# One semaphore for all products of TensorE, and a plan with other costs, in a fused attention and gated feed-forward kernel

## The chip, the cores and the metric

The kernel runs on one core of a Trainium2 chip. The metric is the device time of one execution in microseconds (us), as the median of several runs. Before the change it is 720.37 us, the median of three runs (720.32 to 722.3).

## What is computed

One input x, 2048 rows of 512 numbers in bf16, goes through two branches, and a gate mixes them row by row:

```python
    x = A_x
    g = _sigmoid((x * gate_w).sum(-1, keepdims=True))
    a = _A_ref(x, A_wqkv, A_wo)
    b = _B_ref(x, B_w_gate, B_w_up, B_w_down)
    return g * a + (1 - g) * b
```

Branch a is attention with 32 heads of 16 numbers each, without a mask: q, k and v are products of x with wqkv, the scores of each head are q·k / 4, the softmax runs over all 2048 keys, and the result is multiplied with wo. Branch b is a feed-forward block of width 1376 whose hidden row is the plain product of two projections, (x·w_gate) times (x·w_up), multiplied with w_down.

## The kernel before, in words

**Tiles.** The attention is cut into 2048 score tiles. One tile holds 128 keys against 512 queries for one head, 128 x 512 numbers in one PSUM bank. Four heads and 512 queries make a group `m`; a group has 16 key blocks times 4 heads, 64 tiles, and there are 32 groups. TensorE computes a score tile with four products of 64 rows and 32 columns that run beside each other in one row half of the array (`score`, lines 1173 to 1239, the products on L1219). The other row half (64 rows) works on another tile at the same time. The same form, four products on one row half, serves P·V (`pv_pack`, L1662) and the projections and the feed-forward block ("fills", `tile4`, L554). A few early products use the whole array (L550, L588).

**The exponential** is done in two ways. ScalarE takes most tiles with an ACTIVATE that reads one, two or three neighbouring banks and writes bf16 into cells of the SBUF buffer PT (`act_policy`, lines 1265 to 1323, L1314): a single, a pair or a triple. VectorE takes the others (`dve_pass`, L1378): one TENSOR_SCALAR turns the scores into int16 numbers whose bits, read as bf16, approximate the exponential. To even out the error, three shifted copies of each such tile are made in PT (L1330 on GpSimd, L1331 on VectorE), and P·V runs over all four with V scaled to match. The scaled V copies are made once (L735). Banks 0 to 3 belong to the tiles of ScalarE, banks 4 to 7 to all the rest. `want_d` and `score` decide which engine a tile goes to.

**Other work.** VectorE moves projections out of PSUM (KT L629, QR L686, V L745), multiplies the feed-forward halves (L905, L920), and copies each finished group's P·V result to SBUF (`oraw`, L1601). `norm` (from L1493) then divides by the softmax's sum: the sums go by DMA from `oraw` to `den4`, VectorE takes reciprocals (L1536), a DMA writes them to DRAM (`rscr`), another broadcasts them back into `rb`, and GpSimd multiplies (L1579). The q rows go by DMA from `QR` to `QT` (`q_half`). SP issues nearly all DMAs (L428).

**The order** of all this is made by a planner that is part of the kernel and runs while the program is built. It goes through planned time event by event (the loop from L1857): for each engine that is free, its policy (`act_policy`, `dve_policy`, `pool_policy`, `pe_policy` for each row half, `sp_policy`) picks the next piece of work whose inputs it believes finished. Every piece has a planned cost. `a_cad(n)` is ScalarE's for n neighbouring tiles; each `dma(...)` call is given the time from its issue to its landing; `d_cad`, `d_fast` and `p_cad` are those of VectorE and GpSimd. Some constants steer the choices. `AW` is how long ScalarE may be left idle in the plan for a larger group of tiles. `PW` is how much work VectorE must have ahead before GpSimd takes a shifted copy. `pool_port` and `dve_port` keep GpSimd and VectorE's fast copies apart in planned time. Only the order per engine and the waits survive into the program; the planned times do not.

**The waits** are made in `_Plan.emit` (from L62). Each piece has a stream, which is a semaphore that it increments when somebody needs it. Every other engine has one stream. TensorE's pieces have several: `issue_pe` (L335) makes the stream's name from the kind of product (`pe_s` scores, `pe_pv` P·V, `pe_f` fills, `pe_w` warm-up) and, for products on one row half, the number of the half:

```python
o = P.op("pe", fn, deps, stream + ("" if len(rgs) == 2 else str(rgs[0])), 1, own)
```

For each piece `emit` keeps, per stream, the highest count that its engine is known to have waited for, and leaves out waits that are already covered. What remains is written as one wait per stream ahead of the instruction. The last of them becomes the instruction's own; the others stand ahead of it as separate wait instructions (EVENT_SEMAPHORE), each with one or two semaphores, on the line L96 of `emit`. An exponential of a pair waits for the two score tiles, each in its own stream, and often for the P·V products that last read the cells it will write, in one or two further streams.

Of the kernel before, what the change touches and what calls it, by code (L numbers as in the profile page):

```python
# [17 lines left out]
class _Op:  # L18

    __slots__ = ("eng", "fn", "deps", "stream", "inc", "seq", "count", "waits", "needed", "know", "own", "beg", "vis", "dur", "note")

    def __init__(self, eng, fn, deps, stream, inc):
        self.eng = eng
        self.fn = fn
        self.deps = deps
        self.stream = stream
        self.inc = inc
        self.seq = 0  # L30
        self.count = 0
        self.waits = []
        self.needed = False
        self.know = None
        self.own = []
        self.beg = 0.0
        self.vis = 0.0
        self.dur = 0.0
        self.note = None


class _Plan:
# [9 lines left out]
    def op(self, eng, fn, deps=(), stream=None, inc=1, own=()):  # L52
        o = _Op(eng, fn, [d for d in deps if d is not None], stream or eng, inc)
        self.nstream[o.stream] = o.seq = self.nstream.get(o.stream, 0) + 1
        o.own = [d for d in own if d is not None]
        self.ops.append(o)
        return o

# [3 lines left out]
    def emit(self, nc, stack):  # L62
        know = {}
        for o in self.ops:
            k = know.setdefault(o.eng, {})
            for d in sorted(o.deps + o.own, key=lambda d_: -d_.seq):
                if d.eng == o.eng and d.inc == 1 and d.eng == "pe" and d not in o.own:
                    continue
                if k.get(d.stream, 0) >= d.seq:
                    continue  # L70
                o.waits.append(d)
                d.needed = True
                for s_, v_ in d.know.items():
# [12 lines left out]
        progs = {}  # L86
        for o in self.ops:
            progs.setdefault(o.eng, []).append(o)

        def run(name, eng):  # L90
            for o in progs.get(name, []):
                best = {}
                for d in o.waits:
                    best[d.stream] = max(best.get(d.stream, 0), d.count)
                for s_, v_ in best.items():
                    eng.wait_ge(sems[s_], v_)  # L96
                i = o.fn(eng)
                if o.needed or o.inc == 16:
                    i.then_inc(sems[o.stream], o.inc)

        with nc.Block() as block:  # L101

            @block.gpsimd
            def _(gp):
                run("pool", gp)

            @block.sync
            def _(sy):
                run("sp", sy)

            @block.tensor
            def _(pe):
                run("pe", pe)

            @block.vector
            def _(v):
                run("dve", v)

            @block.scalar
            def _(act):  # L120
                run("act", act)


class _Res:

    __slots__ = ("at", "rel")
# [6 lines left out]
class _Job:  # L133

    __slots__ = ("rank", "dur", "deps", "go", "kind", "alt")
# [45 lines left out]
def _build(nc, A_x, A_wqkv, A_wo, W_gate, W_up, W_down, gate_w, out):  # L181
# [61 lines left out]
    DEL = 5  # L243
    FP = 0
    PACE2 = 1.03
    PW = 0.5
    CQ1 = 1
    WIDE0 = "k"
    XC = 0.26
    AW = 0.2  # L250
    KF = 0

    def a_cad(n):
        return 0.058 + 0.4267 * n

    A_LAT = 0.17

# [17 lines left out]
    with ExitStack() as stack:  # L275
# [56 lines left out]
        def at(t):  # L332
            heapq.heappush(events, t)

        def issue_pe(t, rgs, dur, lat, fn, deps, stream, own=()):  # L335
            o = P.op("pe", fn, deps, stream + ("" if len(rgs) == 2 else str(rgs[0])), 1, own)
            if t < PH and stream != "pe_w":
                dur *= 2
            for r in rgs:
                free[f"pe{r}"] = t + dur  # L340
                busy[f"pe{r}"] += dur
            o.beg = t
            o.dur = dur * len(rgs) / 2
            o.vis = t + dur + lat
            at(t + dur)
            at(o.vis)
            return o
# [299 lines left out]
        def q_half(n, p, src):  # L647
            hs = p
            if n == 0 and p == 0:
                return  # L650
            ops = []
            prev = 2 * n + p - NH
            for jj in range(2):
                for r in range(2):
                    a = 64 * r + 32 * jj + 16 * p
                    dma(
                        0,
                        QT[a : a + 16, hs, jj, :],
                        QR[a : a + 16, :],
                        lambda: src + [o_qz] + (h_last(prev) if prev >= 0 else []),  # L660
                        f"dq{hs}",
                        2.4,
                        ops.append,
                        0.6,
                    )
                    sq[-1].alt = lambda: prev < 0 or prev in q_last
            ev_q[n, p] = ops
# [597 lines left out]
        def act_policy(t):  # L1265
# [9 lines left out]
            if AW and len(fc) > 3:  # L1275
                soon = [u for u in aq if s_op[u].vis <= t + AW]
                if len(soon) > len(rdy):
# [10 lines left out]

                    if grp(soon) > grp(rdy):
                        return False  # L1290
            for n in (3, 2, 1):
                if len(rdy) < n or len(fc) < n:
                    continue
                cand = rdy[: n + 1]
                for sub in itertools.combinations(cand, n):
                    if rdy[0] not in sub:
                        continue
                    us = sorted(sub, key=lambda u: bank_of[u])
                    bs = [bank_of[u] for u in us]
# [9 lines left out]
                    o = issue(  # L1309
                        "act",  # L1310
                        t,
                        a_cad(n),
                        A_LAT,
                        lambda a: a.activation(span(PT, cs).bitcast(BF16), span(ps, bs), ACT.Exp, scale=ESC),  # L1314
                        deps,
                    )
# [89 lines left out]
        def run_copy(eng, t, jb):  # L1406
# [5 lines left out]
            if eng == "dve":  # L1412
                st["dve_port"] = t + dur
                st["port"] = o
            else:
                st["pool_port"] = t + dur
            cq.remove(jb)
            jb.go(o)

# [2 lines left out]
            return min(r, key=lambda j_: j_.rank) if r else None  # L1422

        def pool_policy(t):
            if st["dve_port"] > t + 1e-9:
                return False
            for j_ in sorted(pq, key=lambda j_: j_.rank):
                if vis(j_.deps()) <= t:
                    pq.remove(j_)
                    j_.go(t)  # L1430
                    st["pool_port"] = free["pool"]
                    return True
            jb = next_copy(t)
            if jb is None:
# [58 lines left out]
        def norm(m):  # L1493
# [8 lines left out]
            def after(o):  # L1502
                release(banks[bank], [o])
                o_tail["o", m] = o
                if p == 1:
                    o_tail["mv", m] = []
                    for j in range(4):
# [3 lines left out]
                            oraw[32 * j + 16 : 32 * j + 32, 1, :],  # L1511
                            lambda: [o, o_tail["o", m - 1], o_tail["den", m - 1]],
                            "dmv",
                            2.4,
                            o_tail["mv", m].append,
                            0.6,
                        )
# [4 lines left out]
                    oraw[row0:128:32, p, :].rearrange("j (a b) -> j a b", b=16),  # L1522
                    lambda: [o],
                    f"dden{p}",
                    2.5,
                    dened,
                    0.58,
                )
# [11 lines left out]
            def reced(o2):  # L1540
# [3 lines left out]
                    rec4[:, p, :],  # L1544
                    lambda: [o2, o_tail.get(("rb", m - 2)), o_tail.get(("rb", m - 1)), o_tail.get(("rb", m - 3))],
                    f"drec{p}",
                    2.9,
                    scred,
                    0.55,
                )  # L1550
# [1 line left out]
            def scred(o3):  # L1552
                o_tail["rec", m] = o3
                if p == 1 or single:
# [6 lines left out]
                        return  # L1561
                    mv = o_tail["mv", m]
                    bc = bass.AP(scs.tensor, scs.offset, [[512, 8], [0, 16], [1, 512]])
                    dma(0, rb[:, :], bc, lambda: w + [prev, o_rbz], "drb", 4.2, lambda o: rbed(o, mv), 0.66)

            def rbed(o5, mv=()):
                o_tail["rb", m] = o5
# [313 lines left out]
        for tt in range(4):  # L1881
# [3 lines left out]
                    ps[:, tb[tt], :], idt[:], bsb[:, tt, :], start=True, stop=False, skip_group_check=True  # L1885
                ),
                banks[tb[tt]].rel + [ev_b[c, tt], o_id],
                "pe_f",
            )
        for tt in range(4):  # L1890
            P.op(
# [7 lines left out]
                    skip_group_check=True,  # L1899
                ),  # L1900
                [o_tail["otx"]],
                "pe_f",
            )
        lastpv = npv[last_m, "op"]
        last4 = []
# [10 lines left out]
        for tt in range(4):  # L1916
# [9 lines left out]
            if tt < 2:  # L1926
# [4 lines left out]
                    ps[:, tb[tt], :], olast[:, cs], wol[:, :], start=False, stop=True, skip_group_check=True  # L1931
                ),
                [mt, d_wd["ol"]],
                "pe_f",
            )
            last4.append(o)
        for tt in range(4):
# [52 lines left out]
```

## Time and profile before

| what | value |
|---|---|
| median of three runs | 720.37 us |
| the profiled execution's own time | 719.9 us |
| its span in the profile | 717.7 us |
| granted TensorE clock, mean over the span | 0.998 |
| ScalarE's exponentials | 745 instructions on 1,486 tiles |
| VectorE's exponentials | 562 instructions, one tile each |
| wait instructions on ScalarE / VectorE in the built program | 838 / 434 |

The profile is one execution taken by the hardware profiler. Its first part gives the busy time of each engine: PE is TensorE's products, PEld its weight loads, DVE is VectorE, ACT ScalarE, POOL GpSimd. The group rows give the line, engine, operation, operands and count, then the busy time in us and the mean duration of one in ns, then the idle time just ahead of the group and what ended it. The timeline rows give the start in us from the span's start, the length in us, and how many equal instructions without a gap of some size between them were put into the row. The rows of waits give the waiting engine and line, what it waited for, the us in total, the number of times and the longest. The ends of products are modelled, so a busy TensorE isn't TensorE at its peak.

### The profile page before, as it was taken

Reading aid. Unit: us, or ns where it says so; the run is one execution under the profiler, and the core shown is the slowest. Engines: PE = TensorE matmul, PEld = TensorE weight load, DVE = VectorE, ACT = ScalarE, POOL = GpSimd, SP = SyncE. Lnnn points to the kernel's source line nnn. Section 1 sums busy time; section 2 is a strip of 40 time slices with the busy share of each in tenths; the row PEclk is TensorE's granted clock in tenths of the full one; section 3 lists DMA queues with packets and bytes.
Section 4 is the critical chain, followed back from the end, with each engine's and each line's share of the span. In section 5 each row is a group of like instructions: output and inputs, shape, how many; then the busy total and the mean of one; then the engine's idle time right before and its main releaser. Section 6 shows DMA issues by size and latency. Waiting matters only on the chain.

```text
span 717.7 us, 48228 instructions
## 1 busy us (share of the span) xinstructions
PE 708.9 (99%) x21837; PEld 377.4 (53%) x21842; DVE 670.5 (93%) x1363; ACT 698.3 (97%) x761; POOL 450.1 (63%) x486
## 2 busy tenths in 40 slices
PE   9999999999999999999999999999999999999997
PEld 5445555555454555555555555555555554556542
DVE  6778999999999999999999999999999999999994
ACT  6899999999999999999999999999999999999997
POOL 3235666765757576778756675866656676665571
PEclk9999999999999999999999999999999999999999
DMA  8300112112110041212110142211104321120001
GB/s 242 83 9 7 28 25 53 45 34 59 36 30 5 19 110 37 66 47 61 37 29 26 30 109 50 62 54 42 41 7 95 73 59 43 40 72 7 16 19 39
DMA packets 77629, 34.95 MB, mean 49 GB/s; under 512 B 60784, under 2 KB 74480, under 8 KB 77424
## 3 DMA queue, kind: packets, MB, share of 16 engines
q1 hardware_dynamic: 76624, 31.47, 17.7%
q8 instruction: 171, 2.80, 1.6%
q10 hardware_dynamic: 800, 0.39, 0.2%
q14 instruction: 34, 0.28, 0.1%
HBM read 25.23 MB, written 2.35 MB: 38 GB/s over the span
## 4 chain that ended last, share of the span: by engine, by line
PE 96%; ACT 2%; issue 1%; DVE 0%; DMA 0%; DVEq 0%; ACTq 0%
PE ps L1662 34%; PE ps L1219 34%; PE ps L554 27%; ACT PT L1314 2%; PE ps L550 1%; PE ps L588 1%; PE ps L497 1%; DMA den<-oraw 0%; DVE PT L1378 0%; DVE ost L1950 0%; DVEq L101 0%; ACT KT L1920 0%; ACT KT L1919 0%; DVE KT L1912 0%; DVE OT L1923 0%
## 5 line engine op out<-in xcount | busy, mean ns | idle before, releaser
L1314 ACT ACTIVATE PT<-ps 128x1024 bf16<-128x1024 f32 (+1 forms) x745 | 691.0, 1041 | 9.4 <-PE ps L1219 5.3
L1662 PE MATMUL ps<-PT,VV 64*32 64x512 bf16 x7468 | 554.7, 377 | 0.7
L1330 POOL TENSOR_SCALAR PT<-PT 128x1024 int16<-128x1024 int16 (+1 forms) x442 | 415.2, 965 | 196.7 <-DVE PT L1331 158.2
L1219 PE MATMUL ps<-QT,KT 64*32 64x512 bf16 x8192 | 477.0, 379 | 0.5 <-ACT PT L1314 0.2
L554 PE MATMUL ps<-PT 64*32 64x512 bf16 x5536 | 397.2, 377 | 1.0 <-DVE PT L1378 0.5
L1378 DVE TENSOR_SCALAR PT<-ps 128x512 int16<-128x512 f32 x562 | 369.5, 685 | 15.5 <-PE ps L1219 8.2
L1662 PEld LDWEIGHTS ps<-PT,VV 64*32 64x32 bf16 x7468 | 188.1, 92 | 91.4 <-PE ps L1662 12.6
L1219 PEld LDWEIGHTS ps<-QT,KT 64*32 64x32 bf16 x8192 | 136.9, 89 | 166.2 <-ACT PT L1314 92.2
L1331 DVE TENSOR_SCALAR PT<-PT 128x1024 int16<-128x1024 int16 (+1 forms) x500 | 175.3, 413 | 0.2
L554 PEld LDWEIGHTS ps<-PT 64*32 64x32 bf16 x5536 | 134.8, 92 | 63.5 <-DVE PT L1378 10.7
L554 PE MATMUL ps<-wo,OT 64*32 64x512 bf16 x480 | 35.5, 377 | 0.5 <-issue 0.5
L1579 POOL TENSOR_TENSOR OT<-oraw,rb 128x512 bf16<-128x512 f32 x16 | 20.5, 1279 | 23.6 <-DVE PT L1331 14.3
L735 POOL TENSOR_SCALAR VV<-VV 128x528 bf16<-128x528 bf16 x19 | 12.0, 632 | 35.0 <-DVE VV L745 17.4
L905 DVE CAST usb<-ps 128x512 bf16<-128x512 f32 (+1 forms) x44 | 29.9, 680 | 0.1
L920 DVE TENSOR_TENSOR PT<-ps,usb 128x512 bf16<-128x512 f32 (+1 forms) x44 | 29.9, 680 | 0.0
L1601 DVE COPY oraw<-ps 128x512 f32<-128x512 f32 x31 | 21.2, 684 | 0.8 <-PE ps L1662 0.8
L745 DVE CAST VV<-ps 128x512 bf16<-128x512 f32 x16 | 10.8, 688 | 8.6 <-PE ps L554 8.5
L629 DVE CAST KT<-ps 128x512 bf16<-128x512 f32 x16 | 10.9, 678 | 4.8 <-PE ps L554 2.6
L554 PEld LDWEIGHTS ps<-wo,OT 64*32 64x32 bf16 x480 | 11.3, 91 | 5.9 <-issue 1.0
L969 DVE TENSOR_SCALAR bsb<-ps,omg 128x512 bf16<-128x512 f32 x16 | 11.9, 743 | 0.9 <-PE ps L554 0.8
L613 DVE CAST PT<-ps 128x512 bf16<-128x512 f32 x14 | 8.8, 683 | 2.6 <-PE ps L588 2.6
L686 DVE TENSOR_SCALAR QR<-ps 128x512 bf16<-128x512 f32 x16 | 10.9, 684 | 0.1
(51 smaller groups left out, 76.3 us busy)
## 6 DMA issues: line engine op xcount, KB each, us to landing
PT<-in_B_w_up_dram SPq DMA_DIRECT2D x40, 128.0 KB, 3.1
PT<-in_B_w_gate_dram SPq DMA_DIRECT2D x40, 128.0 KB, 3.2
PT<-in_B_w_down_dram SPq DMA_DIRECT2D x20, 256.0 KB, 2.8
rb<-rscr SPq DMA_DIRECT2D x15, 256.0 KB
QT<-QR SPq DMA_DIRECT2D x124, 16.0 KB, 2.2
oraw<-oraw SPq DMA_DIRECT2D x60, 32.0 KB, 2.2
out_dram<-ost SPq DMA_DIRECT2D x14, 128.0 KB, 1.9
PT<-in_A_x_dram SPq DMA_DIRECT2D x3, 512.0 KB, 7.4
```

The costliest lines, as they stand in the source:

```text
L554: o = pe.matmul(ps[32 * i : min(w, 32 * i + 32), bank, :], lhs(32 * i, min(w, 32 * i + 32))[q], rhs[q], start=s0, stop=s1, tile_position=( ...
L735: return lambda e: e.tensor_scalar(v_cols(k, t), v_cols(0, t), CW[k], 0.0, ALU.mult, ALU.add)
L905: lambda v: v.tensor_copy(usb[0:w, n % 2, :], ps[0:w, bank, :]),
L920: lambda v: v.tensor_tensor(hT[0:w, f, :], ps[0:w, bank, :], usb[0:w, n % 2, :], ALU.mult),
L1219: o_ = pe.matmul(ps[32 * i_ : 32 * i_ + 32, x, :], KT[64 * r : 64 * r + 64, b, kt * 128 + 32 * i_ : kt * 128 + 32 * i_ + 32], QT[64 * r : ...
L1314: lambda a: a.activation(span(PT, cs).bitcast(BF16), span(ps, bs), ACT.Exp, scale=ESC),
L1330: return lambda e: e.tensor_scalar(span(PT, ds), span(PT, cs), 1.0, float(SH[k]), ALU.mult, ALU.add)
L1331: return lambda e: e.tensor_single_scalar(span(PT, ds), span(PT, cs), float(SH[k]), ALU.add)
L1378: lambda v: v.tensor_scalar(span(PT, cs), span(ps, bs), IOFF, 0.0, ALU.add, ALU.max),
L1579: lambda g: g.tensor_tensor(OT[:, pair % 6, :], oraw[:, 0, :], rb[:, :], ALU.mult),
L1601: lambda v: v.tensor_copy(oraw[:, p, :], ps[:, bank, :]),
L1662: o_ = pe.matmul(ps[32 * j : 32 * j + 32, ob, :], v_ap(k, kt, 8 * b + 2 * j + p, p)[rows], PT[rows, cell, :].bitcast(BF16), start=f0, stop ...
```

## The change

It has three parts. First, all of TensorE's pieces go into one stream, "pe"; the old name is kept in a field (`tag`) that makes no instruction. Since counts in one stream follow program order, `emit` now looks at the newest dependency first (`n`, the place in the program, in place of the count within a stream).

Second, the plan's numbers change: `a_cad` is 7.5 ns lower, `AW` is 0.3 in place of 0.2, `PW` 0.4 in place of 0.5, and five kinds of DMA are planned to land 0.4 to 0.7 us later. GpSimd is held back in the plan until VectorE's last port instruction is visible, and VectorE is let go on 0.1 us ahead of GpSimd's end.

Third, ScalarE takes tiles in pairs or singles only (`GM`), never three at once.

```diff
     def op(self, eng, fn, deps=(), stream=None, inc=1, own=()):
...
+        o.n = len(self.ops)
         self.ops.append(o)
...
-            for d in sorted(o.deps + o.own, key=lambda d_: -d_.seq):
+            for d in sorted(o.deps + o.own, key=lambda d_: -d_.n):
...
-    PW = 0.5
+    PW = 0.4
...
-    AW = 0.2
+    AW = 0.3
     KF = 0
+    GM = (2, 1)
 
     def a_cad(n):
-        return 0.058 + 0.4267 * n
+        return 0.0505 + 0.4267 * n
...
-            o = P.op("pe", fn, deps, stream + ("" if len(rgs) == 2 else str(rgs[0])), 1, own)
+            o = P.op("pe", fn, deps, "pe", 1, own)
+            o.tag = stream + ("" if len(rgs) == 2 else str(rgs[0]))
...
                         f"dq{hs}",
-                        2.4,
+                        2.8,
...
-            for n in (3, 2, 1):
+            for n in GM:
...
-                st["pool_port"] = t + dur
+                st["pool_port"] = t + dur - 0.1
+                at(t + dur - 0.1)
...
         def pool_policy(t):
-            if st["dve_port"] > t + 1e-9:
+            if st["dve_port"] > t + 1e-9 or st["port"] is not None and st["port"].vis > t + 1e-9:
                 return False
...
-                    st["pool_port"] = free["pool"]
+                    st["pool_port"] = free["pool"] - 0.1
+                    at(free["pool"] - 0.1)
...
                             "dmv",
-                            2.4,
+                            2.9,
...
                     f"dden{p}",
-                    2.5,
+                    3.2,
...
                     f"drec{p}",
-                    2.9,
+                    3.3,
...
-                    dma(0, rb[:, :], bc, lambda: w + [prev, o_rbz], "drb", 4.2, lambda o: rbed(o, mv), 0.66)
+                    dma(0, rb[:, :], bc, lambda: w + [prev, o_rbz], "drb", 4.8, lambda o: rbed(o, mv), 0.66)
```

The tail's twelve products move from the stream "pe_f" to "pe" as well. Because the planner goes by its costs, the order on every engine is another one after the change. In the built program ScalarE makes 747 exponentials, all pairs, on 1,494 tiles; VectorE takes 554 tiles instead of 562; TensorE has 21,794 products instead of 21,842. TensorE's products increment a semaphore 1,890 times instead of 3,130.

More of the change, by code (lines that the diff above doesn't have):

```diff
@@ L18 @@
 class _Op:
-    __slots__ = ("eng", "fn", "deps", "stream", "inc", "seq", "count", "waits", "needed", "know", "own", "beg", "vis", "dur", "note")
+    __slots__ = ("eng", "fn", "deps", "stream", "inc", "seq", "count", "waits", "needed", "know", "own", "tag", "n", "beg", "vis", "dur", "note")
     def __init__(self, eng, fn, deps, stream, inc):
@@ L35, in __init__ @@
         self.own = []
+        self.tag = ""
+        self.n = 0
         self.beg = 0.0
@@ L1887, in _build @@
                 banks[tb[tt]].rel + [ev_b[c, tt], o_id],
[L1888 removed]
+                "pe",
             )
@@ L1901, in _build @@
                 [o_tail["otx"]],
-                "pe_f",
+                "pe",
             )
@@ L1933, in _build @@
                 [mt, d_wd["ol"]],
-                "pe_f",
+                "pe",
             )
```

## The prediction

> **What bounds the kernel now.** I began with the page's first part, for the share of each engine.
>
> ```profile
> span 717.7 us, 48228 instructions
> PE 708.9 (99%) x21837; PEld 377.4 (53%) x21842; DVE 670.5 (93%) x1363; ACT 698.3 (97%) x761; POOL 450.1 (63%) x486
> ```
>
> Three engines look full. TensorE's 99% is the overlap of pipelined products, so it proves nothing: I looked for its real rate and found this row of the timeline.
>
> ```profile
> 703.71 1.03 PE L1662 MATMUL ps<-PT,VV 64*32 64x512 bf16 x16
> ```
>
> Sixteen products are four groups of four. With the last product's 0.39 us taken off, three further groups took 0.64 us, 0.21 us each, and the two row halves run beside each other. The program has 21,676 such products, 5,419 groups: 5,419 / 2 x 0.214 = 580 us, some 590 us with the wide ones. TensorE has room. So I went to ScalarE, by form, and then to its timeline.
>
> ```profile
> L1314 ACT ACTIVATE PT<-ps 128x1024 bf16<-128x1024 f32 x721 | 669.5, 1044 | 5.3 <-PE ps L1662 1.9 <-PE ps L1219 1.5 <-issue 0.2
> L1314 ACT ACTIVATE PT<-ps 128x1536 bf16<-128x1536 f32 x10 | 14.5, 1450 | 4.0 <-PE ps L1219 3.8
> L1314 ACT ACTIVATE PT<-ps 128x512 bf16<-128x512 f32 x14 | 8.4, 598 | 0.1
> ```
> ```profile
> 9.54 1.94 ACT L1314 ACTIVATE PT<-ps 128x1536 bf16<-128x1536 f32 x2 [1.03 <-PE ps L1219]
> ...
> 25.93 22.86 ACT L1314 ACTIVATE PT<-ps 128x1536 bf16<-128x1536 f32 x25 [0.94 <-PE ps L1219]
> ...
> 379.81 1.03 ACT L1314 ACTIVATE PT<-ps 128x1024 bf16<-128x1024 f32 x1
> ...
> 385.23 2.02 ACT L1314 ACTIVATE PT<-ps 128x1024 bf16<-128x1024 f32 x2
> ...
> 556.76 83.40 ACT L1314 ACTIVATE PT<-ps 128x1024 bf16<-128x1024 f32 x89 [0.31 <-PE ps L1219]
> ...
> 702.41 6.52 ACT L1314 ACTIVATE PT<-ps 128x1024 bf16<-128x1024 f32 x7
> ```
>
> An exponential of a pair lasts 1044 ns, but the next begins before it ends. From 379.81 to 385.23 lie six starts without a wait: 5.42 / 6 = 0.903 us. That is the floor. The 89 from 556.76 on, in one unbroken row, took (83.40 - 1.04) / 88 = 0.936 us. So ScalarE looks busy and still loses 33 ns per pair, in gaps too short for the column of idle time. A triple with its single takes 1.94 us from start to end; less the single's 0.60 us, a triple's step is 1.34 us, and a single's, by the same slope, 2 x 0.903 - 1.34 = 0.46 us.
>
> First start to last start (702.41 + 6.52 - 1.04 = 707.89) is 698.4 us. The floor for it is 721 x 0.903 + 10 x 1.34 + 14 x 0.46 - 0.90 = 670.0 us. **ScalarE sets the end, and 28 us of its stretch are lateness.** The rest, 9.5 us ahead and 9.8 us behind, the change leaves alone.
>
> Why is it late? ScalarE's queue holds separate wait instructions, recorded under one line:
>
> ```profile
> L96 ACTq EVENT_SEMAPHORE  x836: 17/38/1027, 9.4 to 712.8; - x168
> ```
>
> They cost little by themselves (median 38 ns, run while the engine still computes). What matters is which semaphore arrives last. At 14.01 it was the one that the ACTIVATE itself waits for; at 469.36 it was that of a P·V product, for which a separate instruction ahead of it waits:
>
> ```profile
> 13.33 0.62 PE L1219 MATMUL ps<-QT,KT 64*32 64x512 bf16 x12
> ...
> 14.01 1.45 ACT L1314 ACTIVATE PT<-ps 128x1536 bf16<-128x1536 f32 x1 [0.35 <-PE ps L1219]
> ...
> 468.81 0.40 PE L1662 MATMUL ps<-PT,VV 64*32 64x512 bf16 x4
> ...
> 469.36 1.02 ACT L1314 ACTIVATE PT<-ps 128x1024 bf16<-128x1024 f32 x1 [0.23 <-PE ps L1662]
> ```
>
> The first product ends at 13.95 and the exponential starts 0.06 us later; the second ends at 469.21 and it takes 0.15 us. Over all 745 starts, matched to the built program's waits, of those more than 25 ns late: the last arrival was the ACTIVATE's own in 43 (median 52 ns from product to start), a separate wait's in 130 (133 ns behind one wait instruction, 175 behind two). This handover is the term on which the change turns.
>
> **The change part by part.** *One semaphore.* Waits for TensorE collapse into the newest one. In the built programs ScalarE's wait instructions fall from 838 to 120, VectorE's from 434 to 87, and 742 of 749 exponentials carry TensorE's wait themselves. For every late start whose last arrival stood in a separate wait (253 starts over 8 ns late) I took the smaller of its lateness and its excess over 52 ns: they add up to 11.6 us. That is the upper bound, since a handover saved early in a late stretch may be spent waiting for the same product; the lower is 0. Score products wait longest for ScalarE itself, so most of the gain feeds back:
>
> ```profile
> PEld ps L1219 <- ACT PT L1314: 92.2, 384, 0.7
> PEld ps L1219 <- DVE PT L1378: 25.6, 108, 0.5
> PEld ps L1662 <- PE ps L1662: 12.6, 41, 0.6
> PEld ps L554 <- DVE PT L1378: 11.6, 45, 1.0
> PEld ps L554 <- PE ps L554: 4.6, 17, 0.6
> PEld ps L1662 <- DVE PT L1378: 3.3, 12, 0.4
> ```
>
> TensorE waits 92.2 us for ScalarE and 40.5 us for VectorE's passes. I take two thirds, **-8.0 us**.
>
> *Does one count delay anybody?* The two row halves do not always keep program order:
>
> ```profile
> 67.34 0.66 PE L1219 MATMUL ps<-QT,KT 64*32 64x512 bf16 x16
> 67.78 0.60 PE L1662 MATMUL ps<-PT,VV 64*32 64x512 bf16 x8
> ```
>
> In the program the last four of these sixteen scores stand behind the eight P·V products, yet began before them, on the other half. Of 3,294 counting products 50 ended ahead of an earlier one, by 0.13 us on average. With one count, who waits for such a product waits for the earlier ones too: 0 to 50 x 0.13 = 6.4 us. Laid over this trace, it would have moved none of the starts of ScalarE or of VectorE's passes, so I take **0** and keep 6.4 for the range. The Trainium skill (TensorE: Matmul & The Clock Gate, section The mechanism) says that products start and end strictly in program order; by that rule the term's upper end would be 0 too, and one count could never hold anybody up. The trace disagrees in those 50 cases.
>
> *No triples, and the longer wait for a partner (AW).* 747 pairs replace 721 pairs, 10 triples and 14 singles: 747 x 0.903 - 0.90 = 673.6 us against 670.0, **+3.6 us**, since eight more score tiles go to ScalarE (1,494 for 1,486). In return the start-up changes: seven triples with their singles took 25.93 - 9.54 = 16.4 us, floor 12.6. A triple fills three of four banks, and nothing can be scored into them meanwhile; pairs alternate. Between 0 and -3.8; I take **-2.0**, as TensorE is also short of x there.
>
> *Plan costs.* a_cad goes from 0.911 to 0.904 us for a pair, which is the floor. Longer DMAs put consumers later in their queues. What that is worth is seen here:
>
> ```profile
> 418.57 0.26 DVE L1536 RECIPROCAL rec<-den 128x16 f32<-128x16 f32 x1 [0.93 <-DMA den<-oraw]
> ...
> 420.79 3.82 ACT L1314 ACTIVATE PT<-ps 128x1024 bf16<-128x1024 f32 x4 [0.71 <-PE ps L1219]
> ```
>
> The reciprocal stood in VectorE's queue before its denominators had landed; the passes behind it went 0.93 us late, and ScalarE 0.71. In the new order there are 3.8 us of VectorE's work on average between the oraw copy and the reciprocal, where there were 3.2. This one is gone, and perhaps one more: **-0.8** (0 to -2). SP issues the same transfers in the same numbers; only their places among each other move, and no wait is added: GpSimd already waited for VectorE's last port instruction, and the plan now counts with it.
>
> *Who copies.* VectorE makes 554 passes instead of 562 and 28 fewer double shifts, 33 more single ones and 7 more V copies; GpSimd 9 fewer double, 17 more single, 7 fewer V copies. From their rows:
>
> ```profile
> L1378 DVE TENSOR_SCALAR PT<-ps 128x512 int16<-128x512 f32 x562 | 369.5, 685 | 15.5 <-PE ps L1219 8.2 <-PE ps L1662 0.8 <-DVE rec L1536 0.3
> L1331 DVE TENSOR_SCALAR PT<-PT 128x1024 int16<-128x1024 int16 x385 | 151.1, 447 | 0.2
> L1331 DVE TENSOR_SCALAR PT<-PT 128x512 int16<-128x512 int16 x115 | 27.8, 298 | 0.0
> L1330 POOL TENSOR_SCALAR PT<-PT 128x1024 int16<-128x1024 int16 x359 | 366.7, 1045 | 146.0 <-DVE PT L1331 114.2 <-DVE PT L1378 31.7
> ```
>
> By durations VectorE is relieved of 8 x 0.685 + 28 x 0.447 - 40 x 0.298 = 6 us (a V copy taken as a single shift). GpSimd idles 146 us before its doubles alone: later GpSimd copies hide there. ScalarE sees VectorE only through TensorE's 40.5 us of waits: **-1.0**, between -3 and +3, for what an all-new order may do. The end has 48 P·V products behind the last exponential instead of 40: +0.2.
>
> Sum: -8.0 + 0 + 3.6 - 2.0 - 0.8 - 1.0 + 0.2 = -8.0. The profiled execution took 719.9 us (2.2 around its span); the median is 720.37. From the median: **712.4 us**.
>
> **Rivals.** *The floor is reached.* All 11.6, the whole start-up, both DMA waits: -11.6 + 3.6 - 3.8 - 2 - 3 + 0.2 = -16.6, 703.8 us. For it: the gaps are small and the handover is in most of them. Against: 43 late starts already had the short handover.
>
> *TensorE's order paces it.* If late products, not handovers, make the gaps, the saving is spent waiting: 0 + 3.6 - 2.0 - 0.8 - 1.0 + 0.2 = 0, 720.4 us. For it: 43 late starts with the short handover; against: the 92.2 us.
>
> *VectorE holds TensorE up, slower.* TensorE's own budget is 590 + 40.5 (waits for VectorE) + 17.2 (for its own earlier products) = 648 us, against ScalarE's 674. The new plan has no cushion of 7 ns a pair left on ScalarE, and at score tile 1,480 TensorE has 232 products to go where it had 140. If these waits rise by 26 us, TensorE sets the pace; from 50 us (698.4 - 648) the kernel is slower. Were both kinds to double, TensorE's stretch would be 648 + 57.7 = 705.7, 7.3 us over today's: 727.7 us. Against it: 6 us less for VectorE to do.
>
> That the merged wait doesn't reach the ACTIVATE is excluded by the built program, but for seven.
>
> **How the numbers follow.** Forecast (707 to 717.5) 0.58; floor 0.14; TensorE's pace 0.15; VectorE slower 0.13. The range takes in the floor's time and the pace's, and leaves out half of the slower case: 703 to 721. A difference under 0.3% (2.2 us) can't be told from none. Faster: 0.58 + 0.14 + a fifth of the pace case = 0.75; within: 0.11; slower: 0.14.
>
> **What would show it.** Right: pairs in long rows near 0.91 us instead of 0.936; ScalarE's separate waits about 120; the first 28 score tiles done in under 15 us; no reciprocal waiting for den. Wrong: the mean step of a pair unchanged although the waits are gone (TensorE's pace), or TensorE's waits for VectorE's passes well over 40 us (VectorE). A start-up as long as before would take back 2 us; a late q row or rb in the new order would cost what the one at 420.79 did, 0.7 us each.

## The result, and the profile after

The changed kernel takes 716.98 us (median of 13 runs, 714.84 to 720.95) against 720.79 for the kernel before (13 runs beside them). The ratio is 0.9955 with an interval of 0.9937 to 0.9973: 3.2 us faster, between 1.9 and 4.5; the two medians by themselves lie 3.8 us apart. Measured again on another chip the ratio was 0.9936 (0.9912 to 0.996), 4.6 us. The forecast of 712.4 was 8.0 us faster, so the direction held, and the size was 40% of the forecast, 57% in the second measurement. The profiled execution took 716.57 us with a span of 714.7.

The page's first part, and then three rows of the groups by form:

```profile
span 714.7 us, 47027 instructions
PE 704.0 (99%) x21790; PEld 382.6 (54%) x21794; DVE 661.6 (93%) x1367; ACT 696.2 (97%) x763; POOL 447.9 (63%) x487
```
```profile
L1319 ACT ACTIVATE PT<-ps 128x1024 bf16<-128x1024 f32 x747 | 688.9, 1070 | 7.1 <-PE ps L1224 4.2 <-PE ps L1669 1.4 <-PE ps L559 1.2
...
L1383 DVE TENSOR_SCALAR PT<-ps 128x512 int16<-128x512 f32 x554 | 364.1, 683 | 23.0 <-PE ps L1224 16.5 <-PE ps L1669 2.1 <-PE ps L559 0.4
...
L1543 DVE RECIPROCAL rec<-den 128x16 f32<-128x16 f32 x31 | 7.5, 241 | 1.4 <-DMA den<-oraw 1.4
```

The shares say as little as before. The recorded mean of an exponential even rose from 1044 to 1070 ns, although the kernel is faster; only the steps from start to start count. They are in ScalarE's timeline:

```profile
10.15 9.72 ACT L1319 ACTIVATE PT<-ps 128x1024 bf16<-128x1024 f32 x10 [0.85 <-PE ps L1224]
20.11 4.69 ACT L1319 ACTIVATE PT<-ps 128x1024 bf16<-128x1024 f32 x5 [0.24 <-PE ps L1224]
...
81.81 175.64 ACT L1319 ACTIVATE PT<-ps 128x1024 bf16<-128x1024 f32 x191 [0.25 <-PE ps L1669]
...
419.45 174.13 ACT L1319 ACTIVATE PT<-ps 128x1024 bf16<-128x1024 f32 x189 [1.18 <-PE ps L559]
...
622.51 82.78 ACT L1319 ACTIVATE PT<-ps 128x1024 bf16<-128x1024 f32 x90 [0.41 <-PE ps L1224]
```

In the longest row a pair takes (175.64 - 1.04) / 190 = 0.919 us, in the next (174.13 - 1.04) / 188 = 0.921, where it was 0.936: about half of the 33 ns over the floor of 0.903 is gone. The last exponential starts at 622.51 + 82.78 - 1.04 = 704.25, so first to last start is 694.1 us. The floor for 747 pairs is 673.6 (the prediction's), which leaves 20.5 us of lateness where there were 28.4. The span's change closes like this: lateness -7.9, work +3.6, the first exponential 0.6 later (10.15 for 9.54), the part behind the last one 0.6 longer (714.7 - 704.25 = 10.45 for 9.81): -3.0, 717.7 to 714.7.

The wait instructions are gone as built; then the waits that matter:

```profile
L99 ACTq EVENT_SEMAPHORE  x118: 17/17/740, 64.8 to 709.7; - x118
```
```profile
PEld ps L1224 <- ACT PT L1319: 93.4, 387, 0.6
...
PEld ps L1224 <- DVE PT L1383: 17.0, 80, 0.4
DVE PT L1383 <- PE ps L1224: 16.5, 43, 1.1
PEld ps L1669 <- PE ps L1669: 11.8, 39, 0.6
PEld ps L559 <- DVE PT L1383: 9.8, 33, 1.5
...
PEld ps L1669 <- DVE PT L1383: 3.9, 11, 1.2
PEld ps L559 <- PE ps L559: 3.3, 13, 0.4
```

TensorE waits 30.7 us for VectorE's passes (40.5 before), 15.1 for itself (17.2), and as long for ScalarE as before. That last equality hides two opposite effects: the new order with six semaphores (run e2 below) waits 106.3 us for ScalarE, and the order of before with one semaphore (e1) 70.1. An exponential that waits for a P·V product, as the one at 469.36 did before, now starts sooner; the two rows are of TensorE's and of ScalarE's timeline:

```profile
81.33 0.39 PE L1669 MATMUL ps<-PT,VV 64*32 64x512 bf16 x4
```
```profile
81.81 1.02 ACT L1319 ACTIVATE PT<-ps 128x1024 bf16<-128x1024 f32 x1 [0.25 <-PE ps L1669]
```

The product ends at 81.72 and the exponential starts 0.09 us later; before it was 0.15. Over all starts more than 25 ns late (116, where there were 173), all now hang on the ACTIVATE's own wait, with a median of 52 ns from product to start. The handover did what the prediction said; its worth in time was smaller.

### The profile page after: what moved, and what is told of

It reads as the page before. It is cut to its first block, busy times and chain, and to the rows that moved or that the text cites. A ratio compares the mean times of both kernels' runs of the same rounds, so it can differ in the third digit from the quotient of the medians.

```text
span 714.7 us, 47027 instructions
## 1 busy us (share of the span) xinstructions
PE 704.0 (99%) x21790; PEld 382.6 (54%) x21794; DVE 661.6 (93%) x1367; ACT 696.2 (97%) x763; POOL 447.9 (63%) x487
## 4 chain that ended last, share of the span: by engine, by line
PE 94%; ACT 2%; DVE 2%; issue 1%; DMA 0%; DVEq 0%
PE ps L1224 33%; PE ps L1669 32%; PE ps L559 27%; ACT PT L1319 2%; DVE PT L1383 1%; PE ps L593 1%; PE ps L555 1%; PE ps L502 1%; DMA den<-oraw 0%; PE ps L776 0%; DVE VV L750 0%; DVE PT L1336 0%; DVE ost L1957 0%; DVE VV L740 0%; DVE gden L832 0%
## 5 line engine op out<-in xcount | busy, mean ns | idle before, releaser
L1319 ACT ACTIVATE PT<-ps 128x1024 bf16<-128x1024 f32 x747 | 688.9, 1070 | 7.1 <-PE ps L1224 4.2
L1383 DVE TENSOR_SCALAR PT<-ps 128x512 int16<-128x512 f32 x554 | 364.1, 683 | 23.0 <-PE ps L1224 16.5
L1224 PEld LDWEIGHTS ps<-QT,KT 64*32 64x32 bf16 x8192 | 137.5, 89 | 163.0 <-ACT PT L1319 93.4
L1336 DVE TENSOR_SCALAR PT<-PT 128x1024 int16<-128x1024 int16 (+1 forms) x505 | 170.4, 397 | 0.3
L559 PEld LDWEIGHTS ps<-PT 64*32 64x32 bf16 x5536 | 137.5, 92 | 60.2 <-DVE PT L1383 9.1
L559 PE MATMUL ps<-wo,OT 64*32 64x512 bf16 x480 | 37.1, 377 | 0.0
L1586 POOL TENSOR_TENSOR OT<-oraw,rb 128x512 bf16<-128x512 f32 x16 | 20.5, 1282 | 20.6 <-DVE PT L1336 17.8
L740 POOL TENSOR_SCALAR VV<-VV 128x528 bf16<-128x528 bf16 x12 | 7.6, 633 | 29.1 <-DVE VV L750 26.3
```

The source lines that it names most:

```text
L559: o = pe.matmul(ps[32 * i : min(w, 32 * i + 32), bank, :], lhs(32 * i, min(w, 32 * i + 32))[q], rhs[q], start=s0, stop=s1, tile_position=( ...
L1224: o_ = pe.matmul(ps[32 * i_ : 32 * i_ + 32, x, :], KT[64 * r : 64 * r + 64, b, kt * 128 + 32 * i_ : kt * 128 + 32 * i_ + 32], QT[64 * r : ...
L1336: return lambda e: e.tensor_single_scalar(span(PT, ds), span(PT, cs), float(SH[k]), ALU.add)
L1383: lambda v: v.tensor_scalar(span(PT, cs), span(ps, bs), IOFF, 0.0, ALU.add, ALU.max),
L1586: lambda g: g.tensor_tensor(OT[:, pair % 6, :], oraw[:, 0, :], rb[:, :], ALU.mult),
```

## The experiments

Ratios are to the kernel before on the same chip, with 95% intervals. Four groups of runs shared a chip each; the kernel before had a median of 724.07, 723.13, 723.02 and 722.84 us in them, so the expectations that are given in us are read as differences.

| run | what it is | us | ratio |
|---|---|---|---|
| e1_one_sem | before, with one semaphore | 719.56 | 0.9943 (0.9924 to 0.9962) |
| e2_six_sem | after, with six semaphores | 724.93 | 1.0007 (0.9988 to 1.0025) |
| e3_newest_last | before, waits sorted oldest first | 731.48 | 1.0102 (1.0081 to 1.0123) |
| e5_newest_first | before, waits sorted newest first | 721.56 | 0.9977 (0.9953 to 1.0001) |
| e4_twice | after, ScalarE waits twice | 723.14 | 0.9985 (0.9971 to 0.9999) |
| e6_dve_twice | after, VectorE waits twice | 722.78 | 0.9990 (0.9970 to 1.0009) |
| e11_both_twice | after, both wait twice | 724.34 | 1.0026 (1.0009 to 1.0042) |
| a_same | after | 717.46 | 0.9936 (0.9912 to 0.9960) |
| e7_triples | after, groups of three allowed | 730.52 | 1.0116 (1.0085 to 1.0146) |
| e8_short_dma | after, the old landing times | 717.51 | 0.9931 (0.9908 to 0.9954) |
| e10_sp_cost | after, dearer weight issues on SP | 717.29 | 0.9924 (0.9902 to 0.9947) |
| e9_real_loop | after, longer delays planned | 715.55 | 0.9902 (0.9882 to 0.9922) |
| e13_pel | after, one of these delays | 719.49 | 0.9949 (0.9929 to 0.9969) |
| e12_loop_sp | e9 and e10 together | 716.01 | 0.9901 (0.9880 to 0.9922) |

My theory at this point: the semaphore is the whole gain and the plan is worth about nothing, but of the handovers saved most is spent waiting for the next product. The rival: the semaphore gives its full 8 us and the new plan costs 4 or 5.

**The two parts apart.** The order of before with the merged stream alone, and the order of after with six streams:

```diff
 # e1_one_sem, from before (and sorted by n in emit; the tail's products move too)
-            o = P.op("pe", fn, deps, stream + ("" if len(rgs) == 2 else str(rgs[0])), 1, own)
+            o = P.op("pe", fn, deps, "pe", 1, own)
 # e2_six_sem, from after (and sorted by seq in emit; the tail's products move back)
-            o = P.op("pe", fn, deps, "pe", 1, own)
+            o = P.op("pe", fn, deps, stream + ("" if len(rgs) == 2 else str(rgs[0])), 1, own)
```

> The order of before on every engine, with all of TensorE's products in one semaphore and nothing else changed. Handover theory (an exponential whose last arrival stands in a separate wait instruction starts 80 to 120 ns later than one that waits for it itself): 4 to 9 us faster than before, 712 to 717 us, late starts all with a handover near 52 ns. Plan theory (the new order and costs made the gain, the semaphores nothing): within 1.5 us of before, 719 to 722 us.

> The order of the changed kernel on every engine, with the six semaphores of before. Handover theory: the new order alone is no gain, 720 to 726 us, that is 4 to 9 us over the changed kernel, with handovers of 130 to 175 ns at late starts. Plan theory: as fast as the changed kernel, 715.5 to 718.5 us.

The semaphore alone gives -4.1 us (-5.5 to -2.8); the plan alone gives +0.5 (-0.9 to 1.8). They add up to what the whole change does. The rival falls: the plan doesn't take back 4 us, the semaphore gives only half of the forecast.

**What the order of the waits is worth.** Here the streams stay six, and the wait instructions 838; only the order in which the waits ahead of one instruction are written differs, on every engine.

```diff
 # last[s]: the place in the program (n) of the newest product waited for in stream s
-                for s_, v_ in best.items():
+                for s_, v_ in sorted(best.items(), key=lambda b_: last[b_[0]]):   # e3
+                for s_, v_ in sorted(best.items(), key=lambda b_: -last[b_[0]]):  # e5
```

> The order and the six semaphores of before, with as many wait instructions; only the order of the waits ahead of an instruction is changed, so that the newest product in the program is the one that the instruction itself waits for. Handover theory: most of the gain of one semaphore, 3 to 8 us faster than before, 713 to 718 us. Plan theory, and the theory that the number of wait instructions or of increments costs: as before, 719 to 722 us.

> The order of before, the six semaphores of before and the same 838 wait instructions on ScalarE; the waits are sorted the other way round than in the run with the newest last, so that the newest product is the wait of the instruction itself (744 of 747 exponentials, where before has 283 and the run with the newest last 33). Handover theory: as much faster as with one semaphore, 0.992 to 0.997 of before. Theory that the number of wait instructions, semaphores or increments counts: as before, 0.998 to 1.002.

e3 did the reverse of what I meant it to do. In the built programs the wait that is written **first** becomes the instruction's own, not the last, as I had described it above. So in e3 the newest product was the own wait of only 33 of the 747 instructions with which ScalarE reads PSUM into PT (283 before; 745 of the 747 are exponentials, two are copies) and of 198 of VectorE's 562 passes (472 before), and 210 of its 219 late starts had a separate wait arrive last, 133 ns behind one wait instruction and 155 behind two. It cost 7.4 us. e5, with the newest product as own wait of 744 of the 747 and of 555 passes, came to -1.7 us (-3.4 to 0.1), which lies between the two ranges that were expected. Between e3 and e5 lie 1.25%, 9 us, with the same work, the same order of work and the same number of wait instructions: the place of the wait is the cause. Whether the fewer wait instructions and increments of e1 give something besides can't be told, since its interval overlaps e5's. On such instructions the Trainium skill (Perfetto Trace Analysis, section Identifying Dependency Chains) says that instructions waiting on several engines may have EventSemaphore instructions ahead of them; the traces agree, show the same for several semaphores of one engine, and add the price.

**The handover put back.** After, with a second, separate wait for the same count:

```diff
                 for s_, v_ in best.items():
                     eng.wait_ge(sems[s_], v_)
+                    if name == "act" and s_ == "pe":    # e4; "dve" in e6, both in e11
+                        eng.wait_ge(sems[s_], v_)
```

> The changed kernel, where ScalarE waits for the same count of TensorE's semaphore a second time, in a separate wait instruction ahead of each exponential (774 wait instructions on ScalarE instead of 120). Handover theory: 4 to 9 us slower than the changed kernel, 721 to 726 us, handovers of 130 ns or more. Plan theory: as the changed kernel, 715.5 to 718.5 us.

> The changed kernel, where VectorE, not ScalarE, waits a second time for the same count of TensorE's semaphore in a separate instruction (742 wait instructions on VectorE instead of 87). If ScalarE's handover alone makes the gain: as the changed kernel, 0.9935 to 0.9970 of before. If VectorE's handover has a part in it: 0.9975 or more.

> The changed kernel, where ScalarE and VectorE both wait a second time for TensorE's count in a separate instruction. If the two handovers add up (+0.30% for ScalarE alone, +0.35% for VectorE alone): 0.60 to 0.75% over the changed kernel, 1.001 to 1.003 of before, which gives back what one semaphore gained. If they overlap, since a saving on one engine is spent waiting for the other: 0.3 to 0.5% over the changed kernel, 0.998 to 1.000 of before.

> The changed kernel once more, on the same chip as the three beside it: 0.9937 to 0.9973 of before, as first measured.

In e4 the median handover is 112 ns over 158 late starts. One of them, in TensorE's and ScalarE's timeline:

```profile
81.91 0.39 PE L1671 MATMUL ps<-PT,VV 64*32 64x512 bf16 x4
```
```profile
82.46 1.02 ACT L1321 ACTIVATE PT<-ps 128x1024 bf16<-128x1024 f32 x1 [0.24 <-PE ps L1671]
```

From 82.30 to 82.46 it is 0.16 us, where after had 0.09 at 81.72. Over after's two measurements (0.9955, 0.9936) e4 costs 0.30 to 0.49%, e6 0.35 to 0.54%; e11 costs 0.90% over after on the same chip, 6.5 us, more than either theory had. So a separate wait ahead of every instruction costs about the same on either engine, and the two add up. Together they cost more than the change gained, because the kernel before didn't have one everywhere: there 281 of 745 exponentials and 472 of 562 passes already waited for the newest product themselves. Of VectorE's 148 starts in before that stood waiting for a product, 18 had their last increment in a separate wait, with a median of 92 ns from increment to start instead of 24: some 1.2 us in all. How VectorE's reaches the end is in TensorE's waits of e6:

```profile
PEld ps L1226 <- ACT PT L1321: 63.4, 267, 0.5
...
PEld ps L1226 <- DVE PT L1385: 32.3, 132, 0.5
```

TensorE waits 32.3 us for VectorE's passes to free a bank (17.0 in after) and 63.4 for ScalarE (93.4): the loop closes through VectorE more often.

The price at the end is smaller than the sum of the handovers: 158 late starts times 60 ns (112 less 52) would be 9.5 us in e4, if each went on to the end. It took 2.2 to 3.5, a quarter to a third, where 4 to 9 were expected.

**Where the rest of the saving goes.** Before and e1 once more, one execution each on one chip (723.92 and 719.53 us), to lay the starts of the same 745 exponentials side by side:

> The kernel of before once more, for a profile on the same chip as the three beside it. Both theories: as before, within 0.5%.

> The order of before with one semaphore once more, for a profile on the same chip as the kernel of before. Theory of spent savings (a start made earlier waits at the next product, because TensorE's and VectorE's order sets the pace between late starts): the starts of ScalarE gain 10 us or so in some steps and lose more than half of it in others, 3 to 5 us in all. Theory of kept savings: gains without losses, 8 us or more in all.

The first and last rows of ScalarE's exponentials and the waits of TensorE, of b_same:

```profile
9.52 1.94 ACT L1314 ACTIVATE PT<-ps 128x1536 bf16<-128x1536 f32 x2 [1.03 <-PE ps L1219]
...
635.57 77.51 ACT L1314 ACTIVATE PT<-ps 128x1024 bf16<-128x1024 f32 x83 [0.24 <-PE ps L1219]
```
```profile
PEld ps L1219 <- ACT PT L1314: 90.6, 374, 0.7
PEld ps L1219 <- DVE PT L1378: 26.3, 109, 1.0
```

and of e1_again:

```profile
10.21 1.94 ACT L1316 ACTIVATE PT<-ps 128x1536 bf16<-128x1536 f32 x2 [1.03 <-PE ps L1221]
...
587.76 121.14 ACT L1316 ACTIVATE PT<-ps 128x1024 bf16<-128x1024 f32 x131 [0.35 <-PE ps L1221]
```
```profile
PEld ps L1221 <- ACT PT L1316: 71.6, 317, 0.5
PEld ps L1221 <- DVE PT L1380: 26.1, 110, 0.5
```

First to last start falls from 712.04 - 9.52 = 702.5 to 707.86 - 10.21 = 697.7, by 4.9 us. From one exponential to the next, e1 gains 9.1 us on before in steps of under 0.2 us and loses 5.2 in steps as small; the larger ones nearly cancel (-4.0, +2.9). Two executions of one and the same kernel, before and b_same, differ by 1.3 and 2.2 us in the small steps, so these 9.1 and 5.2 are more than chance; their whole stretches differ by 4.2 us, so the 4.9 alone would prove little. TensorE waits 19.0 us less for ScalarE, and no less for VectorE. That is saving and spending: a bank comes free earlier, and then the exponential after it stands at a product that is no earlier. The late starts show the same. In b_same 53 of 189 hang on the ACTIVATE's own wait and are late by 11.7 us together; in e1_again it is 148 of 154 and 26.7 us: the handover is short and the product itself comes late. Which other work holds each such product was not followed one by one.

**The plan's parts.**

```diff
-    GM = (2, 1)                    # e7_triples
+    GM = (3, 2, 1)
 # e8_short_dma: the five landing times of before (2.4, 2.4, 2.5, 2.9, 4.2)
-                    0.42 if n >= NW else 0.6,      # e10_sp_cost, a weight load's issue on SP
+                    0.62 if n >= NW else 0.6,
```

> The changed kernel with groups of three allowed again (GM = (3, 2, 1)); with the new AW the plan then makes 63 triples and 66 singles, all but one of them in the first 132 exponentials, and leaves 581 tiles to VectorE and 1,467 to ScalarE. Theory that pairs alternate and triples do not (the term of 2.0 us for seven triples): 63 triples with their singles at 0.3 to 0.5 us each, less 10 to 12 us for fewer tiles on ScalarE: 8 to 20 us slower than the changed kernel. Theory that triples are neutral: within 2 us of it or faster.

> The changed kernel with the five planned DMA times of before; between the oraw copy and the reciprocal there are then 3.1 us of VectorE's work on average instead of 3.8. Theory that longer planned DMAs save the waits for den (0.8 us forecast): 0.5 to 3 us slower than the changed kernel, and more waits of the reciprocal. Theory that the wait for den comes from SP's queue and stays whatever landing is planned: within 1 us but for the end, where 20 more P·V products follow the last exponential (0.5 us).

> The changed kernel planned with 0.62 us for SP to issue a weight load (0.42 before; the trace shows 0.51 in the median and 1.1 to 1.3 for the slowest tenth). Theory that SP's queue makes the wait for den near 417 us: that wait of 1.4 us is gone, 1 to 2.5 us faster than the changed kernel. Rival: another transfer comes late instead, within 1 us of the changed kernel.

With groups of three allowed the new plan takes 63 of them and is 1.6 to 1.8% slower than after, 12 to 13 us. Over the first 132 exponentials the starts are 29 us late against the floor (4.7 in after), some 0.4 us for each triple, as the first of the two theories had it. ScalarE's timeline shows them one after the other, each with its gap, and ScalarE's waits for scores are 20.4 us where after had 4.2:

```profile
10.34 1.94 ACT L1319 ACTIVATE PT<-ps 128x1536 bf16<-128x1536 f32 x2 [1.03 <-PE ps L1224]
...
131.71 1.94 ACT L1319 ACTIVATE PT<-ps 128x1536 bf16<-128x1536 f32 x2 [0.23 <-PE ps L1224]
```
```profile
ACT PT L1319 <- PE ps L1224: 20.4, 61, 1.0
```

The longer landing times are worth nothing that shows: e8 is as fast as after. The reciprocal that waited 0.93 us before waited 1.39 in after, and this was not the landing. SP's timeline of after, then VectorE's:

```profile
411.73 0.43 SPq L433 DMA_DIRECT2D PT<-in_B_w_up_dram  x1
412.20 0.56 SPq L433 DMA_DIRECT2D PT<-in_B_w_gate_dram  x1
412.81 0.51 SPq L433 DMA_DIRECT2D PT<-in_B_w_up_dram  x1
413.36 1.34 SPq L433 DMA_DIRECT2D PT<-in_B_w_gate_dram  x1
414.74 0.50 SPq L433 DMA_DIRECT2D PT<-in_B_w_down_dram  x1
415.29 0.61 SPq L433 DMA_DIRECT2D den<-oraw  x1
```
```profile
411.01 0.67 DVE L1608 COPY oraw<-ps 128x512 f32<-128x512 f32 x1
...
417.29 0.25 DVE L1543 RECIPROCAL rec<-den 128x16 f32<-128x16 f32 x1 [1.39 <-DMA den<-oraw]
```

The copy ended at 411.68, but the transfer of the denominators was issued only at 415.29: five weight loads stood ahead of it in SP's queue, and their issue took 0.43 + 0.56 + 0.51 + 1.34 + 0.50 = 3.34 us where the plan counts 5 x 0.42 = 2.1. From its issue to its landing it needed 2.0 us. It was the same in before: there the copy ended at 413.28 and the transfer was issued at 416.47, behind weight loads and an output. With 0.62 us planned for each load no reciprocal waits any more; with the old landing times one still does. The group by form in e10, then in e8:

```profile
L1543 DVE RECIPROCAL rec<-den 128x16 f32<-128x16 f32 x31 | 7.5, 242 | 0.0
```
```profile
L1543 DVE RECIPROCAL rec<-den 128x16 f32<-128x16 f32 x31 | 7.5, 242 | 1.1 <-DMA den<-oraw 1.1
```

The time of e10 can't be told from after's, though: a stall of about 1 us is too small for it. The lower `a_cad`, `AW`, `PW` and the rules for the shared port were not tried alone.

**A plan with the loop's measured length.** The plan lets others see a pair's result 0.17 us after ScalarE's step; the duration less the step, 1.044 - 0.903, and 0.05 us until the next weight load starts, make 0.19. A product is planned as visible 0.437 us after its start; the recorded weight load of 0.09, the product's 0.39 and the handover of 0.05 make 0.53.

```diff
-    PEC, PSW, PEL, LEAD = 0.2155, 0.13, 0.437, 0.05
+    PEC, PSW, PEL, LEAD = 0.2155, 0.13, 0.52, 0.05   # e9, e12; 0.50 in e13
-    A_LAT = 0.17
+    A_LAT = 0.20                                     # e9, e12
```

> The changed kernel planned with a longer loop from ScalarE over TensorE and back (A_LAT 0.20 for 0.17, PEL 0.52 for 0.437), nearer to what the trace shows (51 ns from an exponential's end to the weight load, up to 134 more to the product, 390 for it and 52 to the next exponential). Theory that late starts come from a plan that takes this loop too short: lateness falls by 5 us or more, 709 to 714 us on a chip where before takes 720. Theory that any order loses about as much: within 2 us of the changed kernel.

> The changed kernel planned with PEL 0.50 alone (0.437 before). If a plan that leaves products more time is what helps: faster than the changed kernel by 0.2 to 0.6%. If the run with A_LAT 0.20 and PEL 0.52 was only a lucky order: within 0.2% of the changed kernel or slower.

> The changed kernel planned with the longer loop (A_LAT 0.20, PEL 0.52) and SP's longer issue (0.62 us) together. If both costs help by themselves: 0.985 to 0.989 of before. If each new order is a throw of the dice: anywhere from 0.990 to 0.996.

e9 and e12 are the fastest kernels here, 0.9902 and 0.9901, two orders on two chips. e12 is 0.35% under after on its chip, with intervals that overlap a little (0.9922, 0.9912); by the middle of after's two values it is nearer to 0.45%. But the theory behind them isn't borne out. It said that lateness falls by 5 us or more. Reckoned as for after (20.5 us), it is 20.6 us in e9, 20.1 in e12, and 19.8 in e8, which ran on e9's chip with the short delays. What fell in e9 is ScalarE's work:

```profile
L1319 ACT ACTIVATE PT<-ps 128x1024 bf16<-128x1024 f32 x742 | 685.6, 1084 | 6.5 <-PE ps L1224 3.7 <-PE ps L1669 2.0
```
```profile
L1383 DVE TENSOR_SCALAR PT<-ps 128x512 int16<-128x512 f32 x562 | 369.6, 683 | 15.6 <-PE ps L1224 9.4 <-PE ps L559 0.4 <-PE ps L1669 0.3
```

With two singles these 742 pairs are 1,486 tiles, eight fewer than in after; VectorE makes eight passes more. That takes 3.6 us off ScalarE's floor, while the part behind the last exponential is 2.6 us longer (13.1 for 10.45). e13 is 0.13% slower than after on its chip, as the theory of a lucky order said, and e12 lies just inside the range of the dice. So it isn't shown that longer delays help by themselves: each edit also changes the whole order and who takes which tile.

## Why the prediction was right or wrong

**The step that failed is the size of the semaphore's term: "I take two thirds, -8.0 us".** It measured -4.1 us (e1), about a third of the upper bound of 11.6; two thirds of that bound would have been 7.7, not 8.0. The mechanism behind it was right: the late arrivals with a separate wait went from 130 to none, and putting the waits back (e2, e4, e6, e11) or moving them the wrong way (e3) takes time each time. What was wrong is how much of a handover reaches the end. I argued from TensorE's 92.2 us of waits for ScalarE that a handover saved feeds back into the next score. It does, but then the start after it stands at a product that is no earlier: 9.1 us gained in small steps, 5.2 lost again. The rival "TensorE's order paces it" had the right cause and, at 720.4, claimed too much of it; the measured 717.0 lies between it and the forecast. I had given it 15%, with the 43 starts of short handover as the only evidence. The bound of 11.6 us also counts ScalarE alone. That error is small: VectorE had some 1.2 us to save in before.

**Does one count delay anybody: 0.** Right, and for a stronger reason than I gave. The 50 early products go by the products' ends, which are modelled. The recorded times of the semaphores' increments say otherwise: in the trace of before all 3,294 increments (not the 3,130 stated with the change) come in program order, although they belong to several streams, and so they do in e2, e3 and e5. A score product shown to end at 408.00 raised its semaphore at 408.48 only, and the exponential that waits for it started at 408.50; no exponential of before starts sooner than 23 ns behind the last increment it waits for. So the upper end of this term was 0, not 6.4 us, and "the trace disagrees" in the prediction doesn't hold for what a waiting engine sees. The times fit: e1, with one count, is at least as fast as e5, which keeps six and has the newest wait in the same place (intervals overlap).

**Work +3.6** follows from the counts, and the span's change closes with it. **Start-up -2.0**: the 15th pair starts at 20.11 + 4.69 - 1.04 = 23.76, so the first 28 tiles took 13.6 us instead of 16.4; with the first start 0.6 later that is -2.2. I hadn't foreseen the later start. e7 confirms that triples are dear.

**The den wait, -0.8: wrong, and its cause with it.** I read a late landing and expected "this one is gone". The wait grew to 1.39 us and ScalarE's gap from 0.71 to 1.18, because SP's queue issued late, as it had in before; I had counted its transfers as unchanged and not looked at when they were issued.

**VectorE, -1.0**: in the direction, TensorE's waits for its passes fell by 9.8 us, and by 9.5 in e2, so this is the order's doing; what it gave at the end was not isolated. **Tail +0.2** was 0.6. **The sum of the plan's terms was forecast as 0.0 and measured as +0.5**, right within its interval, though it hides the errors above. The slower case, VectorE holding TensorE up, didn't come: those waits had to rise and fell.

## What to carry to other kernels

When an instruction waits for several things, see which wait ends up in the instruction itself, and make it the one that arrives last; merging an engine's semaphores does that, and so, partly, does the order in which the waits are written. In a tight loop of engines count only a part of the sum of the handovers saved, here a quarter to a third, unless the engine that waits is shown to be the only one that paces it. When a planner's cost changes, see first who does which work in the new order, and only then credit the cost. Look at the issuing queue before you call a late transfer slow.

## What the runs showed of the hardware that was not expected

- A separate wait instruction whose own record is 17 (e4) to 38 ns (before) long in the median costs a late start 60 ns (e4, same semaphore) to 120 ns (175 against 52, two instructions).
- TensorE's increments come in program order across all its semaphores (3,294 of 3,294 in before), also where the profile shows the end of a product up to 0.5 us ahead of its increment.
- SP takes 0.51 us in the median to issue a load of `w_gate`, but up to 1.6:

```profile
L433 SPq DMA_DIRECT2D PT<-in_B_w_gate_dram x44: 474/508/1615, 16.9 to 589.3; - x44
```

- The kernel before had medians from 720.79 to 724.07 us in the five groups of runs, which differ by as much as the change itself; only ratios to the kernel before of the same group can be used.
